# Another order for a fused RWKV-6 and feed-forward kernel

## The chip, the cores and the metric

The kernel runs on one core of one Trainium2 chip. The metric is the device time of one execution in microseconds, the median of several runs. A core has a matmul engine (PE, with its weight loads shown apart as PEld), a vector engine (DVE), a scalar engine (ACT), a further vector-like engine (POOL) and a queue that issues the transfers (SP). Each of them works through its own list in order; semaphores tie the lists together.

## What is computed

Two stages. The first is a linear attention with a decaying state: for each batch (4) and head (8) and each of 768 time steps, with vectors of length 48,

```python
cur   = einsum('bhd,bhe->bhde', u * k_t, v_t)
y_t   = einsum('bhd,bhde->bhe', r_t, state + cur)
state = w_t * state + einsum('bhd,bhe->bhde', k_t, v_t)
```

The second takes the 3072 tokens of 8 x 48 = 384 values and computes `maximum(x @ w1, x @ w2) @ w_out`, with 1024 inner columns.

## The kernel before

The time axis is cut into three segments of 256 steps, and the work into eight **units**: units 0 to 3 are segment 0 of one batch each, units 4 and 5 segment 1 of two batches each, units 6 and 7 segment 2 of two batches each. A unit's state feeds the unit of the next segment (0 and 1 feed 4, 2 and 3 feed 5, 4 feeds 6, 5 feeds 7).

A unit's chain, by the names that the order uses: `load` brings r, k, v, w. `wp` multiplies neighbouring decays, `ln` takes the logarithm, `ex` sums it along time on PE (from unit 3 on with the value split into two half-precision parts by `hi` and `lo`), `mz`, `e0` and `ie` make from it the factors that scale r and k. `rw`, `kw` weight r and k by the neighbour's decay; `scale.u.0` makes the scaled r, `scale.u.1` the scaled k. `rk`, `ru`, `dg`, `dd`, `di` make the diagonal term with u. The scaled r and k are turned by PE and copied back (`tr`, `te`: units 0 to 4) or by a DMA transpose (`dt`: units 5 to 7). `sc` multiplies k with r on PE in many small matmuls, `mk` is a masked copy of the result on DVE, `ya` multiplies it with v (rows of 32 small matmuls of 64x32), `yi` adds the state's part (12 or 24 small matmuls), `kv`, `st`, `sm`, `sb` update the state, `xe` copies the finished y out of PSUM as bf16 input of the second stage.

The second stage is rewritten: since `maximum(a, b) = relu(a - b) + b`, the kernel makes `wd = w1 - w2` (`wload`, then `wdiff` for each of three row blocks) and the product `w2 @ w_out` (`woload`, `wocast`, `w2turn`, `w2take`, `wfold`, `wctake`). Then `gt` is one PSUM bank of `x @ wd` (three matmuls of 512 columns, or six of 256 for units 0 to 3), `rl` its relu, `op` the output product of 128 tokens (11 matmuls of 384 columns), `oe` the copy out of PSUM, `os` the store. `hot` is a filler: matmuls on zeros, from the start's idle time.

There is no automatic scheduling. `ORDER` (line 53) is one written list of 652 entries; each is a function's name, the unit, further indices, and after `@` the engine where there is a choice (`d` DVE, `a` ACT, `p` POOL). The kernel calls the functions in that order (line 755), so it fixes the order within each engine's list, and by the buffers that rotate also who waits for which buffer. PSUM has four banks of the kind `G` (`ex`, `tr`, `gt`, `op`) and two double banks `Y` (`kv`, `sc`, `y`).

Lines that the steps touch: `hot` L234, `zero` L249 to L263, `w_diff` L176/L180, `w2_turn` L307, `load` L372, `ex` L395 to L398, `mz` L440, `dg` L502, `di` L516, `tr` L565, `dt` L582, `kv` L596, `sc` L641, `mk` L650, `yi` L675, `ya` L688, `gt` L706, `rl` L717/L719, `op` L725 and L729, `os` L743. Products and copies run through helpers at L176, L180 and L168.

Of the kernel before, what the change touches and what calls it, by code (L numbers as in the profile page):

```python
# [59 lines left out]
vb.0.0@p ln.2.0 we.1.0 ex.2.0 vb.0.1@a load.2.r scale.0.0.0.1@d di.0.0@d wload.1.0 te.0.0.0@a  # L60
wload.1.2 we.0.1 ie.1.0 rk.1.0@d kv.0 kw.1.0@d hot.8.4 tr.0.0.1 ru.1.0@d st.0.0@a dg.1
scale.1.1.0.0@p vb.1.1@a kv.1 e0.1.0 mz.2.0 scale.1.0.0.0@d dd.1@p te.0.0.1@a wload.0.2 st.1.0@a
tr.1.0.0 sb.1.1@a tr.1.0.1 ie.2.0 load.3.w.0 wload.0.0 sb.0.1@a zero.M.0@p rk.2.0@d st.0.1 wload.1.1
kw.2.0@p rw.2.0@d sc.0.0.1.0 st.1.1 zero.v.0@d w2turn.2.1 sb.0.0@a w2take.2.1@a e0.2.0 sc.0.0.0.0
di.1.0@d te.1.0.1@a scale.2.0.0.0@d sc.0.0.0.1 hot.8.1 mk.0.0.1.0 mk.0.0.0.0 sc.0.0.1.1 load.3.k
# [6 lines left out]
rl.1.3@a rl.0.3@a kw.3.0@p gt.1.1 gt.0.2 di.2.0@d rw.3.0@p rl.1.1@a vb.2.0@a gt.0.0 rl.0.0@a  # L72
mk.2.0.0.0 woload.2 kv.2 st.2.0@a rl.0.2@a sc.2.0.1.0 w2take.1.0@a sb.2.0@a sb.2.1@a ru.3.0@d gt.0.1
rl.0.1@a mk.2.0.1.0 woload.3 wocast.3@a gt.1.0 load.4.w.0 sm.1@p rl.1.0@a dg.3 wocast.1@p wocast.2@p
dd.3@p ex.3.0 mz.3.0 ie.3.0 e0.3.0 gt.1.2 rl.1.2@a di.3.0@d yi.2.0 ya.2.0.1.0 ya.2.0.0.0 wp.4.0@d
ln.4.0 hi.4@a wfold.1 wfold.2 wfold.0 wctake.1@a load.4.k scale.3.0.0.0@d scale.3.1.0.0@p tr.3.0.1
load.4.r load.3.v wctake.2@a st.2.1 wctake.0@a tr.3.0.0 rk.4.0@d te.3.0.1@a vb.3.1@p op.1.1
# [6 lines left out]
di.4.1@d mk.4.1.0.0 tr.4.0.0 gt.3.0 rl.2.1@a te.4.0.1@a mk.4.1.1.0 wp.5.0@p ln.5.0 gt.3.3 hi.5@a
lo.5@d load.5.r vb.4.0@p kv.4 st.4.0 rl.3.0@a gt.2.3 rl.3.3@a te.4.0.0@a rl.2.3@a gt.3.1 os.0.0
rk.5.0@p rk.5.1@p kw.5.0@p sb.4.1@a rw.5.0@p ru.5.0@d op.2.0 st.4.1 load.6.r oe.2.0@a sc.4.0.0.0
load.5.v sc.4.0.1.0 row.4 op.2.1 ex.5.0 sb.4.0@a di.4.0@d mk.4.0.1.0 rl.3.1@a ya.4.1.1.0 load.6.v
wl.4 ex.5.1 gt.3.2 mk.4.0.0.0 mz.5.0 oe.2.1@a e0.5.0 os.1.1 mz.5.1 wp.6.0@d scale.5.0.0.0@d load.6.k
# [12 lines left out]
rl.5.1@a sb.6.0@a dt.6.1.0 ex.7.0 mz.7.0 mk.6.1.0.0 rl.5.4@a ex.7.1 dt.6.0.0 mz.7.1 op.5.2 load.7.v
e0.7.0 sc.6.0.0.0 mk.6.0.0.0 sc.6.0.1.0 rk.7.1@p mk.6.0.1.0 ie.7.0 wl.5 os.3.0 op.5.3 rk.7.0@p
kw.7.0@p rw.7.0@d oe.5.2@a sb.6.1@a yi.6.0 ya.6.0.0.0 ya.6.1.0.0 scale.7.1.0.0@p os.5.2 dt.7.1.0
ya.6.1.1.0 ya.6.0.1.0 oe.5.3@a ru.7.0@d yi.6.1 e0.7.1 ru.7.1@p scale.7.0.0.0@d dt.7.0.0 op.5.1
vb.7.1@a xe.6.0@a xe.6.1@a dg.7 op.5.0 oe.5.1@a dd.7@a di.7.1@d oe.5.0@a os.4.2 scale.7.1.1.0@p
dt.7.1.1 gt.6.3 os.4.3 gt.6.4 os.5.0 gt.6.0 scale.7.0.1.0@d rl.6.0@a vb.7.0@d sc.7.0.1.0 gt.6.2
# [691 lines left out]
```

## Time and profile before

| | |
|---|---|
| median of three runs | 152.28 us (152.27 to 152.72) |
| the profiled execution | 151.69 us |
| its span, first to last instruction | 150.0 us |
| PE busy | 137.2 us |
| DVE busy | 115.9 us |
| POOL busy | 93.9 us |
| ACT busy | 89.8 us |
| moved by the DMA engines | 31.85 MB |

Line numbers in a row are those of the kernel; `out<-in` are the program's tile names; `x` is a count. A bracket at the end of a timeline row gives the idle time of that engine just before it, and what ended it; "issue" is idle time in which the engine waited for nothing that the profile shows. Matmuls overlap in PE, so distances from start to start say more than the duration of one. A row of a table of stretches gives for each engine the busy time and, in brackets, the number of its instructions, then the clock granted to PE.

### The profile page before, as it was taken

How to read it: one execution, taken by the hardware profiler on the slowest of the kernel's cores; microseconds unless marked ns; L12 is line 12 of the kernel's file. 1: busy time of each engine (PE TensorE's matmuls, PEld its weight loads, DVE VectorE, ACT ScalarE, POOL GpSimd, SP SyncE). 2: the span in 40 equal slices, each digit the busy share in tenths (PEclk: the TensorE clock that was granted, in tenths of full speed). 3: DMA queues.
4: the chain of work that ended last, by engine and by line, in shares of the span. 5: the costliest groups of instructions: out<-in, count | busy, mean ns of one | idle time of the engine just before them, and what ended most of it. 6: DMA issues, size and time to landing. Idle time of an engine off the chain costs nothing. (4 is left out here: it accounts for less than half of the span.)

```text
span 150.0 us, 5536 instructions
## 1 busy us (share of the span) xinstructions
PE 137.2 (91%) x2402; PEld 84.8 (57%) x2404; DVE 115.9 (77%) x155; ACT 89.8 (60%) x167; POOL 93.9 (63%) x110
## 2 busy tenths in 40 slices
...
GB/s 107 322 317 293 376 377 388 326 317 290 286 197 256 182 261 205 240 267 265 202 211 218 241 245 195 54 242 208 221 145 74 238 184 2 111 57 157 4 52 160
DMA packets 71187, 31.85 MB, mean 212 GB/s; under 512 B 66293, under 2 KB 70390, under 8 KB 71162
## 3 DMA queue, kind: packets, MB, share of 16 engines
...
q8 instruction: 19, 0.31, 1.0%
...
## 5 line engine op out<-in xcount | busy, mean ns | idle before, releaser
L706 PE MATMUL G<-xT,wd_sb 128*128 128x256 bf16 (+1 forms) x192 | 35.0, 329 | 0.7 <-DVE rp L176 0.6
L729 PE MATMUL G<-wo_sb,gT 128*128 128x384 bf16 x192 | 35.1, 326 | 0.0
L650 DVE CAST_PREDICATED M<-mask,Y 128x1024 bf16<-128x1024 int32 (+1 forms) x26 | 28.7, 1132 | 5.3 <-PE Y L641 4.9
L717 ACT ACTIVATE gT<-G 128x512 bf16<-128x512 f32 x41 | 23.2, 599 | 14.1 <-PE G L706 13.9
L729 PEld LDWEIGHTS <-gT 128*128 128x128 bf16 x192 | 18.8, 98 | 12.4
L706 PEld LDWEIGHTS <-wd_sb 128*128 128x128 bf16 x192 | 18.3, 99 | 13.2 <-issue 1.3
L180 POOL TENSOR_TENSOR rku<-rku,u_b 128x384 f32<-128x384 f32 x12 | 15.7, 1330 | 3.6 <-DVE rku L176 3.6
L180 POOL TENSOR_TENSOR kp<-lk,iE 128x384 bf16<-128x384 f32 x16 | 16.3, 1038 | 2.6 <-ACT iE L460 1.5
L725 PE MATMUL G<-wc_sb,xT 128*128 128x384 bf16 x72 | 15.7, 328 | 0.0
L234 PE MATMUL G<-S_b 128*128 128x512 bf16 x46 | 12.8, 424 | 2.5 <-DVE S_b L263 2.1
L168 ACT COPY RK<-G 128x1024 bf16<-128x1024 bf16 x12 | 11.7, 1012 | 3.2 <-PE G L565 3.2
L168 ACT CAST xT<-Y 128x768 bf16<-128x768 f32 x8 | 8.1, 1029 | 7.6 <-PE Y L688 4.6
L688 PE MATMUL Y<-M,vp 64*32 64x128 bf16 x768 | 9.9, 223 | 2.9 <-issue 2.9
L641 PE MATMUL Y<-RK 48*64 48x128 bf16 x384 | 9.7, 225 | 2.8 <-DMA RK<-kp 1.8
L502 DVE TENSOR_REDUCE dg<-rku 128x16 f32<-128x768 f32 x12 | 11.1, 948 | 1.0 <-POOL rku L180 0.7
L168 ACT CAST S_b<-S_f 64x192 bf16<-64x192 f32 (+1 forms) x15 | 8.6, 574 | 4.6 <-DVE S_f L612 4.3
L641 PEld LDWEIGHTS <-RK 48*64 48x64 bf16 x384 | 6.3, 108 | 8.0 <-issue 4.6
L688 PEld LDWEIGHTS <-vp 64*32 64x32 bf16 x768 | 7.4, 91 | 5.6 <-issue 4.8
L176 POOL TENSOR_TENSOR S_f<-T,W 128x192 f32<-128x192 f32 (+1 forms) x6 | 4.4, 738 | 8.9 <-ACT W L488 8.9
L516 DVE TENSOR_TENSOR M<-identq,gd 128x512 int32<-128x512 int32 x12 | 9.7, 810 | 0.3 <-ACT gd L168 0.3
L234 PEld LDWEIGHTS <-S_b 128*128 128x128 bf16 x48 | 5.0, 107 | 8.6 <-issue 2.6
L176 DVE TENSOR_TENSOR rp<-lr,G 128x768 bf16<-128x768 f32 (+2 forms) x11 | 8.7, 800 | 0.8 <-POOL lk L180 0.7
...
## 6 DMA issues: line engine op xcount, KB each, us to landing
lk<-in_k_dram SPq DMA_DIRECT2D x12, 384.0 KB, 5.2
lv<-in_v_dram SPq DMA_DIRECT2D x12, 384.0 KB, 6.4
lr<-in_r_dram SPq DMA_DIRECT2D x10, 384.0 KB, 5.3
lw<-in_w_dram SPq DMA_DIRECT2D x9, 384.0 KB, 4.4
...
gT<-in_moe_w_dram SPq DMA_DIRECT2D x4, 512.0 KB, 8.9
...
wso<-in_moe_w_out_dram SPq DMA_DIRECT2D x4, 384.0 KB, 6.2
```

The source lines that it names most:

```text
L168: (nc.scalar.copy if e == "a" else nc.vector.tensor_copy if e == "d" else nc.gpsimd.tensor_copy)(o, i)
L176: op(o, a, b)
L180: op(o[:, g], a[:, g], b[:, g])
L234: nc.tensor.matmul(t, zz[:, 0:P], zz[:, 0:512], start=True, stop=True)
L502: nc.vector.reduce_sum(s.dg[:, b].rearrange("p i h -> p h i"), s.rku[:, b], axis=AX.X)
L641: nc.tensor.matmul(t[q * Q:(q + 1) * Q, e, p * P:(p + 1) * P].rearrange("s (i g) -> s i g", i=2), s.kT[d, b, j, y * n + p, q, :], s.rT[d, ...
L650: nc.vector.copy_predicated(t[:, :, 2 * n * y:2 * n * (y + 1)].rearrange("s i (p e) g -> s p e i g", e=2), mask[:, j].bitcast(I32).unsquee ...
L688: nc.tensor.matmul(lhsT=s.vp[g, b, 2 * p + e, j, m * 32:(m + 1) * 32], rhs=s.M[b, j][g, :, 2 * p + e, :], **into(s, b, q, p * 96 + (e + m) ...
L706: nc.tensor.matmul(t[:, m * n * P:(m + 1) * n * P].rearrange("c (b t) -> c b t", t=P), wd_sb[:, ko, fo * P:(fo + 1) * P], s.xT[:, 0:n, ko, :],
L717: nc.scalar.activation(o, i, AF.Relu)
L725: nc.tensor.matmul(t[:, 0:HD], s.xT[:, a, ko, :], wc_sb[:, ko, :], start=(ko == 0), stop=False)
L729: nc.tensor.matmul(t[:, 0:HD], s.gT[:, c:c + P], wo_sb[:, f, :], start=False, stop=(f == FO - 1))
```

## The change

Only `ORDER` is replaced. All 652 entries are there again, with the same names and indices; their sequence differs from the first entry on, the loads included, and 66 entries carry another engine letter: 13 go from POOL to DVE, 8 from DVE to POOL, 17 from ACT to DVE, 15 from DVE to ACT, 5 from ACT to POOL and 8 from POOL to ACT. In several places `op` or `gt` entries now stand between the `yi` and `ya` rows of a unit (for instance `op.2.1` and `op.3.0` among those of unit 4, `op.4.2` and `op.4.3` between `yi.5.0` and `yi.5.1`). The lists, cut to the parts that are spoken of:

```diff
 ORDER = """
-load.0.r load.0.k zero.r@d zero.s.1@p zero.s.0@d zero.M.1@p load.0.w.1 ident zero.m@p hot.8.2 mask
-zero.k.1@p load.0.w.0 tri wp.0.1@d rw.0.1@d wp.0.0@d ln.0.0 hot.8.3 ex.0.0 identb@p rk.0.0@d
-load.1.w.0 u zero.o@p uspread kw.0.1@d mz.0.0 ln.0.1 ex.0.1 mz.0.1 utake@a ru.0.0@d load.1.k
...
-ya.0.0.1.0 wload.0.1 woload.0 load.2.v zero.M.2@p ya.0.0.0.0
-w2take.0.1@a wocast.0@p wdiff.1@d ya.1.0.0.0 yi.1.0 ln.3.0 ya.1.0.1.0 load.3.r w2turn.1.0 vb.2.1@p
-xe.1.0@a sm.0@p woload.1 yi.0.0 ya.0.0.0.1 zero.v.2@d row.2 w2take.1.1@a ru.2.0@d ya.0.0.1.1
-xe.0.0@a dg.2 hi.3@a sc.2.0.0.0 trih@a gt.1.3 lo.3@d w2turn.0.0 gt.0.3 dd.2@a w2take.0.0@a rk.3.0@d
...
-sc.3.0.0.0 mz.4.0 kv.3 e0.4.0 gt.2.0 mz.4.1 st.3.0@a ru.4.1@p sb.3.0@a op.0.1 load.4.v mk.3.0.0.0
-rl.2.0@d sc.3.0.1.0 scale.4.0.0.0@d ie.4.0 e0.4.1 scale.4.0.1.0@d op.1.0 wl.3 oe.0.1@a oe.1.0@a
-kw.4.0@p scale.4.1.0.0@p we.3 wl.2 gt.2.2 load.6.w.0 ru.4.0@p st.3.1 we.2 scale.4.1.1.0@d tr.4.1.1
-te.4.1.1@a sm.2@p tr.4.1.0 te.4.1.0@a vb.4.1@p op.0.0 ya.3.0.0.0 mk.3.0.1.0 ya.3.0.1.0 dg.4 oe.0.0@d
...
-ru.5.1@p rl.3.2@a dg.5 vb.6.1@a ie.5.0 op.3.0 scale.5.1.0.0@p yi.4.0 yi.4.1 dt.5.0.0 dd.5@p ln.6.0
-ya.4.0.0.0 ya.4.0.1.0 xe.4.0@a ya.4.1.0.0 xe.4.1@d oe.3.0@a e0.5.1 row.5 os.1.0 os.0.1 hi.6@a op.3.1
-gt.4.5 vb.5.1@a scale.5.1.1.0@p scale.5.0.1.0@d os.2.1 rl.4.5@a gt.4.4 oe.3.1@a di.5.1@d lo.6@d
-gt.4.3 gt.4.2 gt.4.0 rl.4.4@a dt.5.1.0 sc.5.0.1.0 we.4 sm.4@p sc.5.0.0.0 rl.4.3@a rl.4.0@a dt.5.0.1
...
-ya.5.0.0.0 sc.5.1.0.0 op.4.2 scale.6.0.0.0@d ie.6.0 e0.6.1 mk.5.1.0.0 wp.7.0@p yi.5.1 load.7.k
-yi.5.0 ya.5.1.0.0 ya.5.0.1.0 scale.6.0.1.0@d dt.6.0.1 ya.5.1.1.0 op.4.1 dg.6 load.7.r xe.5.1@d
...
+load.0.w.0 zero.m@p zero.o@p load.1.w.0 tri zero.s.0@d hot.8.2 hot.8.3 load.0.r mask ident wp.0.0@p
+ln.0.0 ex.0.0 rw.0.0@d zero.M.1@p zero.k.0@d zero.k.1@p u uspread zero.v.2@d load.0.w.1 wp.0.1@d
+wp.1.0@d ln.1.0 rw.0.1@d load.0.k rk.0.0@d mz.0.0 ln.0.1 ex.0.1 utake@a hot.8.0 mz.0.1 ie.0.1
+load.0.v vb.0.0@d identq@a identb@p kw.0.1@p wt.0.0 e0.0.1 ex.1.0 wt.0.1 ru.0.0@d zero.r@d load.1.k
+zero.s.1@p kw.1.0@d hot.8.5 load.2.w.0 dg.0 vb.0.1@a ie.0.0 kw.0.0@p we.0.0 e0.0.0 scale.0.1.0.0@p
...
+te.1.0.0@a sc.1.0.1.0 st.1.1 woload.2 scale.2.0.0.0@d sm.1@d row.2 wload.0.1 wp.3.0@p kw.2.0@p
+sb.0.1@a scale.2.1.0.0@p tr.2.0.0 tr.2.0.1 wocast.2@a w2turn.2.0 sc.1.0.0.0 te.2.0.1@a sb.1.1@d
+w2turn.1.1 w2take.1.1@a te.2.0.0@a di.1.0@d mk.1.0.1.0 ya.1.0.1.0 yi.1.0 mk.1.0.0.0 wdiff.1@d
+ya.1.0.0.0 ya.0.0.0.1 ya.0.0.1.1 woload.1 wload.0.2 wocast.1@a wdiff.2@d w2turn.1.0 ru.2.0@d dg.2
+xe.1.0@a load.3.r zero.M.2@p ya.0.0.1.0 ln.3.0 yi.0.0 wdiff.0@p gt.1.2 w2take.2.0@a load.2.v
+load.3.k gt.1.3 ya.0.0.0.0 w2take.1.0@a gt.1.0 rl.1.3@d hi.3@p lo.3@d sc.2.0.1.0 woload.3 sm.0@d
+vb.2.0@a vb.2.1@p rl.1.2@a dd.2@a gt.1.1 xe.0.0@a trih@a gt.0.2 ex.3.0 rk.3.0@d rl.1.1@a rl.1.0@a
...
+rl.0.0@a wl.2 mz.4.1 e0.4.1 ya.2.0.1.0 rk.4.1@d vb.3.0@p kv.3 op.0.1 ya.2.0.0.0 mz.4.0 st.3.0@a
+sb.3.0@a sb.3.1@a st.3.1 we.2 rw.4.0@d scale.4.0.1.0@d kw.4.0@d ie.4.0 oe.0.1@a ru.4.0@p sm.2@p
+xe.2.0@a op.1.1 gt.2.0 e0.4.0 scale.4.0.0.0@d sc.3.0.1.0 load.5.w.0 scale.4.1.1.0@d oe.1.1@a
+ru.4.1@p load.4.v vb.4.1@p wp.5.0@p vb.4.0@a sc.3.0.0.0 mk.3.0.0.0 gt.2.2 rl.2.2@a op.1.0 tr.4.1.0
+ya.3.0.0.0 te.4.1.0@a ln.5.0 tr.4.1.1 oe.1.0@a mk.3.0.1.0 ya.3.0.1.0 te.4.1.1@a row.4 hi.5@a yi.3.0
...
+load.6.v rk.5.1@d wl.4 mk.4.0.0.0 mk.4.0.1.0 rl.2.3@a op.2.0 oe.2.0@a gt.3.2 ie.5.0 ya.4.1.0.0 we.4
+op.2.1 rl.3.2@a e0.5.1 e0.5.0 ya.4.0.0.0 wp.6.0@d ya.4.0.1.0 ya.4.1.1.0 load.6.k rk.5.0@p rw.5.0@p
+scale.5.0.1.0@d vb.5.1@a op.3.0 load.6.r oe.2.1@a yi.4.0 kw.5.0@p scale.5.1.0.0@p vb.5.0@a yi.4.1
+ln.6.0 hi.6@a xe.4.0@a xe.4.1@a scale.5.0.0.0@d ru.5.1@d ru.5.0@d op.3.1 dg.5 gt.4.6 gt.4.4 dt.5.0.0
+oe.3.1@d dd.5@a gt.4.7 rl.4.6@a di.5.0@d sm.4@p gt.4.0 dt.5.1.0 sc.5.0.0.0 sc.5.0.1.0 rl.4.7@a
...
+rl.4.3@a op.4.0 oe.4.0@d sc.5.1.0.0 sb.5.1@a mk.5.1.0.0 ya.5.0.0.0 yi.5.0 mz.6.0 mz.6.1 vb.6.1@a
+ie.6.0 e0.6.1 load.7.k os.1.0 rw.6.0@p ru.6.0@d e0.6.0 load.7.r op.4.2 op.4.3 dg.6 yi.5.1 kw.6.0@p
+scale.6.1.1.0@p ya.5.1.1.0 ya.5.0.1.0 ya.5.1.0.0 oe.4.3@d os.2.0 scale.6.0.0.0@d dt.6.1.1
...
+gt.7.4 rl.7.4@a gt.7.6 rl.7.6@a gt.7.3 rl.7.3@a gt.7.5 rl.7.5@d op.7.2 oe.7.2@a os.7.2 op.7.3
+oe.7.3@a op.7.1 oe.7.1@d op.7.0 oe.7.0@d os.7.3 os.7.1 os.7.0
 """.split()
```

More of the change, by code (lines that the diff above doesn't have):

```diff
@@ L60 @@
[L60 to L65, printed above, removed]
@@ L66 @@
-mk.0.0.1.1 zero.v.1@d te.1.0.0@a sc.1.0.0.0 scale.2.1.0.0@p tr.2.0.0 mk.0.0.0.1 sb.1.0@a wdiff.2@p
-tr.2.0.1 te.2.0.1@a mk.1.0.0.0 w2turn.1.1 te.2.0.0@a wdiff.0@p sc.1.0.1.0 mk.1.0.1.0 w2turn.0.1
-w2turn.2.0 w2take.2.0@a wp.3.0@d ya.0.0.1.0 wload.0.1 woload.0 load.2.v zero.M.2@p ya.0.0.0.0
-w2take.0.1@a wocast.0@p wdiff.1@d ya.1.0.0.0 yi.1.0 ln.3.0 ya.1.0.1.0 load.3.r w2turn.1.0 vb.2.1@p
-xe.1.0@a sm.0@p woload.1 yi.0.0 ya.0.0.0.1 zero.v.2@d row.2 w2take.1.1@a ru.2.0@d ya.0.0.1.1
-xe.0.0@a dg.2 hi.3@a sc.2.0.0.0 trih@a gt.1.3 lo.3@d w2turn.0.0 gt.0.3 dd.2@a w2take.0.0@a rk.3.0@d
@@ L72 @@
[L72 to L77, printed above, removed]
@@ L84 @@
[L84 to L88, printed above, removed]
-ru.5.1@p rl.3.2@a dg.5 vb.6.1@a ie.5.0 op.3.0 scale.5.1.0.0@p yi.4.0 yi.4.1 dt.5.0.0 dd.5@p ln.6.0
@@ L101 @@
[L101 to L106, printed above, removed]
@@ new lines @@
+zero.v.0@d load.1.r scale.0.0.0.0@d mz.1.0 wt.1.0 scale.0.1.0.1@p ie.1.0 load.2.r rk.1.0@d wp.2.0@d
+kv.0 load.2.k st.0.0@a we.1.0 dd.0@p di.0.0@d zero.M.0@p wload.1.0 rw.1.0@d sb.0.0@a tr.0.0.0 e0.1.0
+te.0.0.0@a load.1.v hot.8.4 ru.1.0@d we.0.1 w2turn.0.1 w2take.0.1@a sc.0.0.0.0 scale.0.0.0.1@d
+tr.0.0.1 ln.2.0 scale.1.1.0.0@p sc.0.0.1.0 dg.1 load.3.w.0 scale.1.0.0.0@d tr.1.0.1 vb.1.1@d
+te.0.0.1@a st.0.1 rk.2.0@d ex.2.0 mz.2.0 mk.0.0.0.0 vb.1.0@p mk.0.0.1.0 sc.0.0.1.1 wload.1.2
+w2turn.0.0 te.1.0.1@a w2take.0.0@d tr.1.0.0 sc.0.0.0.1 mk.0.0.1.1 e0.2.0 ie.2.0 w2turn.2.1
@@ new lines @@
+w2take.2.1@a dd.1@a kv.1 st.1.0@a sb.1.0@a wload.0.0 hot.8.1 mk.0.0.0.1 wload.1.1 rw.2.0@p
+te.1.0.0@a sc.1.0.1.0 st.1.1 woload.2 scale.2.0.0.0@d sm.1@d row.2 wload.0.1 wp.3.0@p kw.2.0@p
[3 more added lines that the diff above has]
+xe.1.0@a load.3.r zero.M.2@p ya.0.0.1.0 ln.3.0 yi.0.0 wdiff.0@p gt.1.2 w2take.2.0@a load.2.v
@@ new lines @@
+load.3.k gt.1.3 ya.0.0.0.0 w2take.1.0@a gt.1.0 rl.1.3@d hi.3@p lo.3@d sc.2.0.1.0 woload.3 sm.0@d
+vb.2.0@a vb.2.1@p rl.1.2@a dd.2@a gt.1.1 xe.0.0@a trih@a gt.0.2 ex.3.0 rk.3.0@d rl.1.1@a rl.1.0@a
+kw.3.0@p di.2.0@d mk.2.0.1.0 rl.0.2@a sc.2.0.0.0 mk.2.0.0.0 mz.3.0 woload.0 wocast.0@a rw.3.0@p
+gt.0.3 ru.3.0@d load.4.w.0 rl.0.3@a wocast.3@p gt.0.1 rl.0.1@a wp.4.0@d kv.2 st.2.0@a dg.3 load.3.v
+e0.3.0 scale.3.0.0.0@d ie.3.0 zero.v.1@d wfold.0 wfold.2 wfold.1 st.2.1 sb.2.0@a sb.2.1@a load.4.r
+scale.3.1.0.0@p tr.3.0.1 wctake.0@a dd.3@d ln.4.0 hi.4@a row.3 wctake.2@a wctake.1@a vb.3.1@a
@@ new lines @@
+te.3.0.1@a yi.2.0 lo.4@d di.3.0@d tr.3.0.0 load.4.k te.3.0.0@a ex.4.0 rk.4.0@d gt.0.0 ex.4.1
+rl.0.0@a wl.2 mz.4.1 e0.4.1 ya.2.0.1.0 rk.4.1@d vb.3.0@p kv.3 op.0.1 ya.2.0.0.0 mz.4.0 st.3.0@a
[3 more added lines that the diff above has]
+ya.3.0.0.0 te.4.1.0@a ln.5.0 tr.4.1.1 oe.1.0@a mk.3.0.1.0 ya.3.0.1.0 te.4.1.1@a row.4 hi.5@a yi.3.0
@@ new lines @@
+dg.4 dd.4@d wl.3 di.4.0@d xe.3.0@a scale.4.1.0.0@p we.3 op.0.0 oe.0.0@d gt.2.1 tr.4.0.1 sc.4.1.1.0
+sc.4.1.0.0 di.4.1@d load.5.k gt.3.3 load.5.r rl.2.0@a rl.2.1@a tr.4.0.0 te.4.0.1@a load.6.w.0
+te.4.0.0@a os.0.0 lo.5@d mk.4.1.1.0 load.5.v gt.3.0 rl.3.0@a rl.3.3@a mk.4.1.0.0 kv.4 st.4.0 ex.5.1
+ex.5.0 sm.3@p mz.5.1 sb.4.0@a gt.3.1 gt.2.3 rl.3.1@a st.4.1 sc.4.0.1.0 sb.4.1@d mz.5.0 sc.4.0.0.0
+load.6.v rk.5.1@d wl.4 mk.4.0.0.0 mk.4.0.1.0 rl.2.3@a op.2.0 oe.2.0@a gt.3.2 ie.5.0 ya.4.1.0.0 we.4
+op.2.1 rl.3.2@a e0.5.1 e0.5.0 ya.4.0.0.0 wp.6.0@d ya.4.0.1.0 ya.4.1.1.0 load.6.k rk.5.0@p rw.5.0@p
```

35 lines of the change are left out of this document (17 added, 18 removed).

## The prediction

> **What bounds the kernel now.** I read the page first, then the stretches between landmarks, then PE's waits, then the timeline around each.
>
> ```profile
> span 150.0 us, 5536 instructions
> PE 137.2 (91%) x2402; PEld 84.8 (57%) x2404; DVE 115.9 (77%) x155; ACT 89.8 (60%) x167; POOL 93.9 (63%) x110
> ...
> q8 instruction: 19, 0.31, 1.0%
> ```
>
> ```profile
> core 0: us, PE busy (x) PEld busy (x) DVE busy (x) ACT busy (x) POOL busy (x), PEclk, DMA share, GB/s
> 6.22:31.20 24.98, 22.35 (x336) 14.14 (x337) 23.87 (x44) 16.23 (x38) 19.89 (x26) 1.00 1.12 341
> 31.20:60.20 29.00, 27.74 (x448) 19.35 (x447) 24.93 (x32) 22.98 (x45) 21.21 (x23) 0.94 0.97 249
> 60.20:146.80 86.60, 82.92 (x1609) 49.73 (x1608) 66.17 (x80) 48.78 (x83) 47.42 (x46) 1.00 0.72 166
> 146.80:150.00 3.20, 0.00 (x0) 0.00 (x0) 0.00 (x0) 0.48 (x1) 0.00 (x0) 0.84 0.50 184
> ```
>
> Two regimes. From 6.22 (the first product of w) to 31.20 (the last weight difference) DVE is the full engine: 23.87 of 24.98 us. From 60.20 (the first `ya` of unit 3) to 146.80 it is PE: 82.92 of 86.60, while DVE has 20 us to spare. The last 3.20 us are the last copy and its store. PE's real waits after the start are three:
>
> ```profile
> 35.38 1.26 PE L706 MATMUL G<-xT,wd_sb 128*128 128x256 bf16 x6
> 60.22 0.75 PE L688 MATMUL Y<-M,vp 64*32 64x128 bf16 x64
> 83.65 0.64 PE L641 MATMUL Y<-RK 48*64 48x128 bf16 x32 [1.81 <-DMA RK<-kp]
> 96.97 0.31 PE L688 MATMUL Y<-M,vp 64*32 64x128 bf16 x14 [1.07 <-issue]
> 118.73 0.81 PE L706 MATMUL G<-xT,wd_sb 128*128 128x512 bf16 x3 [0.65 <-DVE rp L176]
> ```
>
> 1.81 us for a DMA transpose of unit 5, 1.07 us for nothing that the profile shows ("issue") inside unit 5's `ya` rows, 0.65 us for a PSUM bank that DVE held. Together 3.53 us.
>
> **What "issue" is.** The same wait stands in the start, also inside a `ya` row:
>
> ```profile
> 32.36 0.40 PE L688 MATMUL Y<-M,vp 64*32 64x128 bf16 x26 [1.83 <-issue]
> ...
> 0.00:32.10 32.10, 26.50 (x346) 15.72 (x349) 25.74 (x48) 17.52 (x39) 26.16 (x44) 1.00 1.04 313
> 0.00:96.70 96.70, 88.08 (x1625) 57.16 (x1628) 83.00 (x113) 67.25 (x128) 79.79 (x97) 0.98 0.96 256
> 0.00:26.30 26.30, 22.27 (x220) 12.39 (x222) 19.94 (x38) 14.19 (x34) 20.36 (x39) 1.00 1.03 311
> 0.00:74.00 74.00, 68.00 (x1115) 45.16 (x1118) 63.31 (x91) 51.19 (x102) 60.27 (x77) 0.98 1.01 274
> 0.00:76.30 76.30, 70.30 (x1241) 46.84 (x1245) 65.47 (x94) 53.48 (x104) 62.57 (x79) 0.98 1.00 271
> ```
>
> Queue q8 moves 0.31 MB in 19 pieces, 16 KB each; 4,806 PE and weight-load records over 19 are 253 for a piece. At the first stall 346+349 = 695 records had run, at the second 1625+1628 = 3253: the distance is 2558, ten times 256 less two. So I read the stalls as PE running out of instructions at the end of a block of 256. Block ends then lie at 695 and every 256 records before and after it. The block before the first stall began at record 439, just before 26.30 (442), so it lasted 6.1 us to 32.36. The block before the second began at 2997, when the `yi` row at 94.19 started; it lasted 2.8 us to 96.97. One block ran through without a wait in 2.3 us (records 2231 at 74.00 to 2487 at 76.30), so there is no fixed limit; I use 2.8 us where the loads are light and 6.1 us in the start.
>
> A rule speaks against this reading. The Trainium skill, Runtime: NRT & Kernel Launch, section Instruction fetch mechanics, has the same blocks of 256 instructions, but calls their refill hidden, since instructions are dispatched more slowly than they are filled. The trace agrees on the size, and shows two stalls of 1.83 and 1.07 us where it expects none. By the page the second is something else and stays in the new order: that is a rival below.
>
> **The change, part by part.** No instruction is added or removed: both orders have the same 652 entries, and PE has the same matmuls. What changes is position, and the engine of 66 entries.
>
> *Engines.* With the row means of before, 30 entries move onto DVE (13 from POOL, 17 from ACT) with 20.3 us, 23 leave it with 16.6: DVE 115.9 becomes some 119.6. POOL loses some 13 us, ACT gains some 3.
>
> *Instruction blocks.* Counting the new PE order in the same way, the block with unit 5's rows now holds most of `op.4.2`, all of `op.4.3`, then `yi.5.1` and three `ya` rows: 0.9+1.9+0.4+1.1 = 4.3 us at least (`op` from the rows below, 92.30 to 94.19; 32 `ya` matmuls 0.36 us, 91.59 to 91.95), against 2.8 needed. Unit 4's block holds `op.3.0` between its rows, 3.2 us. So the 1.07 us go.
>
> ```profile
> 91.59 0.42 PE L688 MATMUL Y<-M,vp 64*32 64x128 bf16 x32
> 91.95 0.42 PE L641 MATMUL Y<-RK 48*64 48x128 bf16 x16
> 92.30 0.66 PE L725 MATMUL G<-wc_sb,xT 128*128 128x384 bf16 x3
> 92.80 1.46 PE L729 MATMUL G<-wo_sb,gT 128*128 128x384 bf16 x8
> 94.19 0.86 PE L675 MATMUL Y<-RK,S_b 128*32 128x128 bf16 x48
> ```
>
> *Transposes.* On SP `dt.5.1.0` stood behind `row.5` and three stores; now it follows `dt.5.0.0` directly.
>
> ```profile
> 75.18 1.75 SPq L582 DMA_TRANSPOSE RK<-rp  x1
> 76.98 0.41 SPq L472 DMA_DIRECT2D row<-MZ  x1
> 77.44 1.26 SPq L743 DMA_DIRECT2D out_dram<-osb  x2
> 78.82 1.29 SPq L743 DMA_DIRECT2D out_dram<-wb  x1
> 80.22 1.26 SPq L582 DMA_TRANSPOSE RK<-kp  x1
> ```
>
> It was issued at 80.22 and let PE go at 83.65, 3.4 us later. Its place in the new order is worked out after the next part.
>
> ```profile
> lk<-in_k_dram SPq DMA_DIRECT2D x12, 384.0 KB, 5.2
> ...
> gT<-in_moe_w_dram SPq DMA_DIRECT2D x4, 512.0 KB, 8.9
> ```
>
> *Loads.* Counted in pieces of these two sizes, the last feed-forward weight now has 8.64 MB ahead and with it instead of 8.25; 0.39 MB at 341 GB/s are 1.1 us. DVE, not this load, is later (below), so I cost it at nothing; uncovered it is 1.1 us.
>
> *The start, by DVE.* The first feed-forward matmul needs all of `wdiff`. DVE's first need is now `load.0.r`, with 0.2+0.4+0.4 MB before and in it; that is what stood before and in the half of w that started DVE at 6.22, so it starts there again. From its row means the old list to `wdiff.1` (38 entries) sums to 25.9 us and took 24.98; the new one to `wdiff.2` (43 entries, `wdiff.2`, two more `vb`, a `w2take`, `sm.1` and `sb.1.1` among them) sums to 28.3. In the old proportion, 28.3 x 24.98/25.9 = 27.3: done at 33.5. Without any wait 28.3 x 23.87/25.9 = 26.1: 32.3. The first `gt` follows at 33.5 rather than 35.38.
>
> *The middle, by DVE.* What I did not expect to find: between that point and PE's `ya.3.0.0.0` the new order puts more on DVE than on PE.
>
> ```profile
> 29.99 1.21 DVE L176 TENSOR_TENSOR wd_sb<-gT 128x1024 bf16<-128x1024 f32 x1
> 36.35 0.56 DVE L413 SCALAR_TENSOR_TENSOR wst<-lg,wst 128x384 f16<-128x384 f32 x1 [2.66 <-ACT wst L200]
> 51.01 1.02 DVE L440 TENSOR_TENSOR MZ<-G,lg 128x384 f32<-128x384 f32 x2 [0.36 <-PE G L396]
> 51.95 1.22 DVE L650 CAST_PREDICATED M<-mask,Y 128x1024 bf16<-128x1024 int32 x1
> ```
>
> ```profile
> L502 DVE TENSOR_REDUCE dg<-rku 128x16 f32<-128x768 f32 x12 | 11.1, 948 | 1.0 <-POOL rku L180 0.7
> L176 DVE TENSOR_TENSOR rku<-lr,lk 128x768 f32<-128x768 f32 x8 | 8.6, 1079 | 0.0
> ```
>
> With the means of the view by shape (two of its rows stand here), the 22 entries of before from 31.20 to the end of `mk.3.0.0.0` at 53.17 sum to 19.7 us; less its waits of about 3.2 the stretch took 18.8 (factor 0.95). PE needed that mask only at 60.22, so DVE was 7 us early. Now 30 entries lie there (`kw.4.0`, both scalings of r and one of k of unit 4, a `rl`, `sm.0`, `st.3.1` and more ahead of the mask): 25.4 x 0.95 = 24.1 us. The mask ends at 33.5+24.1 = 57.6, with 0.7 us of waits (the old ones without the 2.66, whose cause, `hi.3` on ACT, moves to POOL) at 58.3. PE's own work between the first `gt` and `ya.3.0.0.0` is 22 us (the old 24.84 us for what was 2.3 more, `op.0.0` and a `tr`, and partly at a lower clock): it arrives near 55.5 and waits. So the start's gain is eaten: at 58.3 PE stands 2.3 us of work earlier in its list than before at 60.22.
>
> *From there to the end.* Before: 146.80-60.22 = 86.58, less 3.53 of waits 83.05, plus the 2.3 us not yet done: 85.35. `dt.5.1.0` is issued after `scale.5.0.0.0`, 20 DVE entries or 17.3 us after 58.3, plus 1.3 us for `dt.5.0.0`: 76.9, landing 80.3. PE took 83.65-1.81-60.22 = 21.6 us from the first `ya` of unit 3 to the `sc` row that waited; the new list has the 2.3 us more and one `gt` (some 0.7) less, so it comes at 58.3+23.2 = 81.5: no wait, margin about 1 us. For waits of PE on DVE I take 1.7 us: what PE waited for DVE in all of before, by these rows, bounded by 0.4 us (`mk.3.0.1.0` follows the first mask, 1.2 us against 0.8 us of PE work) and 3.5 (all that was won).
>
> ```profile
> PE Y L641 <- DVE M L650: 0.7, 1, 0.7
> PE G L706 <- DVE rp L176: 0.6, 1, 0.6
> PE Y L641 <- DVE T L615: 0.4, 1, 0.4
> ```
>
> *Sum.* 58.3 + 85.35 + 1.7 + 3.2 (the tail; its last copy goes to DVE, within 0.1 us) = 148.55, against the span of 150.0: 1.45 us less. The profiled execution took 151.69, so 150.2; the median of the runs is 152.28, 0.6 above it, so **150.8**. Its own range, with DVE's waits from 0 to 1.5 us, is 149.6 to 151.9.
>
> **The rivals.**
>
> *DVE loses nothing:* no waits in start or middle. The mask ends at 32.3+24.1 = 56.4, with 0.4 of waits later: 56.4+85.35+0.4+3.2 = 145.35, so 147.6. For it: DVE stood 95% full there before. Against: it waited 3.2 us in the middle even so.
>
> *The transposes are late again:* the margin of 1 us is lost and the 1.81 us return: 152.6, no change. For it: in both orders `dt.5.1.0` stands right before the `sc` rows that read it, with four `gt` ahead now and five then. Against: no store stands between the two transposes any more.
>
> *The page's rule:* the 1.07 us were unit 5's rows themselves and not instructions: 151.9, no change. Against it stands the distance of 2558 records.
>
> *Slower: DVE is the bound from the start to unit 3.* Every wait of DVE up to `mk.3.0.0.0` is now paid in full, since PE stands behind that mask. With the 3.2 us of before, and 0.5 us because a block end now falls into `ya.0.0.0.1` (that block begins near 26.8, plus 6.1 is 32.9, then 1.5 us of PE work to the first `gt`, which `rl.1.3` on DVE awaits): 33.5+0.5+24.1+3.2 = 61.3, end 151.55, so 153.8. It decides from 2.2 us of waits on. For it: the lists above, and the clock row, 0.94 granted between 31.20 and 60.20 after a stall of that kind. Against: 2.66 of the 3.2 had a cause that moves.
>
> **How the numbers follow.** A run of this kernel can't be told from no change within 0.3%, 151.8 to 152.7. Chances: forecast 0.42, no waits 0.14 (faster, 0.56); late transposes 0.13 and the page's rule 0.06 (same, 0.19); DVE the bound 0.25 (slower). The range leaves out the ends: 147.9 to 153.9.
>
> **What would show it.** Right: no "issue" wait of PE over 0.3 us after 40 us; no wait of PE on RK near 80; a PE wait of 1 to 3 us on DVE's mask before the first `ya` of unit 3, near 56 to 59; first `gt` between 33 and 35; DVE near 119.6 busy. Wrong: the first `gt` after 36, a wait for `wd_sb` on a load, or PE waits for DVE above 3 us in the second half.

## The result, and the profile after

| | runs | median, us | lowest to highest, us |
|---|---|---|---|
| before | 6 | 152.28 | 151.78 to 152.72 |
| after | 6 | 150.38 | 149.82 to 151.65 |

The new order takes 0.9892 of the time of the old one, with a 95% interval of 0.9846 to 0.9937: 1.6 us, or 1.9 between the medians. The forecast was 150.8. Now and then an execution of a kernel is disturbed and takes a per cent or more longer: ratios, here and below, leave these executions out and medians keep them, so the two need not agree.

Beware of setting the two profiles side by side. The profiled execution of before (151.69 us, span 150.0) was faster than all of its six runs, that of after (151.65 us, span 149.8) the slowest of its six. The spans differ by 0.2 us where the medians differ by 1.9. What they can show is where the time lies, and there they differ a lot. First the page of after, then its stretches, cut where PE starts the first `ya` of unit 3 (60.22 before, 60.13 here) and where PE ends.

```profile
span 149.8 us, 5513 instructions
PE 139.4 (93%) x2402; PEld 84.7 (56%) x2404; DVE 118.8 (79%) x162; ACT 93.4 (62%) x168; POOL 85.4 (57%) x98
```

```profile
6.32:35.17 28.85, 25.05 (x367) 15.51 (x367) 27.34 (x49) 18.06 (x38) 18.48 (x21) 0.92 0.98 308
0.00:34.30 34.30, 28.82 (x346) 16.59 (x348) 27.17 (x49) 18.83 (x38) 23.88 (x42) 0.95 0.93 287
0.00:62.30 62.30, 55.98 (x858) 34.77 (x860) 53.07 (x83) 41.28 (x82) 43.13 (x60) 0.95 0.93 267
60.13:146.60 86.47, 85.06 (x1629) 51.00 (x1627) 67.38 (x81) 54.16 (x90) 44.43 (x42) 1.00 0.80 179
```

DVE's total of 118.8 us is close to the 119.6 that was counted. From the first `ya` of unit 3 to PE's end it took 86.47 us against 86.58 before, but with some 2.3 us more work in it. So the second half won some 2.2 us, and in these two profiles the start lost about as much: PE came to unit 3 at the same moment with 2.3 us less behind it.

The timeline of PE in after shows both. Columns are start, us, what ran, and in brackets the idle time before it and what ended that.

```profile
31.83 0.43 PE L688 MATMUL Y<-M,vp 64*32 64x128 bf16 x32 [1.24 <-DVE M L650]
...
32.96 0.48 PE L688 MATMUL Y<-M,vp 64*32 64x128 bf16 x34 [0.42 <-DVE M L650]
34.41 0.82 PE L688 MATMUL Y<-M,vp 64*32 64x128 bf16 x30 [0.97 <-issue]
...
37.09 1.66 PE L706 MATMUL G<-xT,wd_sb 128*128 128x256 bf16 x12
...
60.13 0.42 PE L688 MATMUL Y<-M,vp 64*32 64x128 bf16 x32
...
62.38 0.23 PE L675 MATMUL Y<-RK,S_b 128*32 128x128 bf16 x1 [0.64 <-issue]
...
84.38 0.64 PE L641 MATMUL Y<-RK 48*64 48x128 bf16 x32
...
92.51 0.65 PE L725 MATMUL G<-wc_sb,xT 128*128 128x384 bf16 x3
...
94.29 0.65 PE L725 MATMUL G<-wc_sb,xT 128*128 128x384 bf16 x3
...
96.63 1.03 PE L688 MATMUL Y<-M,vp 64*32 64x128 bf16 x96
97.60 0.66 PE L725 MATMUL G<-wc_sb,xT 128*128 128x384 bf16 x3
...
103.89 0.64 PE L641 MATMUL Y<-RK 48*64 48x128 bf16 x32 [0.36 <-DMA RK<-rp]
```

The first `gt` came at 37.09, 1.7 us later than before, not 1.9 us earlier as forecast. Ahead of it PE waited 1.24 and 0.42 us for DVE's masks and 0.97 us for instructions, at record 346+348 = 694. From there to 60.13 PE waited no more than 0.16 us at a time, and the forecast wait for unit 3's mask isn't there. The wait for the transpose (84.38) and the issue wait in unit 5's rows (96.63, all 96 matmuls in one piece) are gone. One issue wait of 0.64 us is new, at record 858+860 = 1718, in unit 3's `yi` row. With 0.36 us at 103.89 and 0.32 us at 125.98 the second half has 1.3 us of waits instead of 3.53.

### The profile page after: what moved, and what is told of

Its sections match the earlier page's. It is cut to its first block, busy times and chain, and to the rows that moved or that the text cites. A ratio compares the mean times of both kernels' runs of the same rounds, so it can differ in the third digit from the quotient of the medians.

```text
span 149.8 us, 5513 instructions
## 1 busy us (share of the span) xinstructions
PE 139.4 (93%) x2402; PEld 84.7 (56%) x2404; DVE 118.8 (79%) x162; ACT 93.4 (62%) x168; POOL 85.4 (57%) x98
## 4 chain that ended last, share of the span: by engine, by line
PE 75%; DVE 13%; DMA 6%; issue 3%; ACT 1%; DVEq 0%; ACTq 0%
PE G L729 20%; PE G L706 17%; PE G L725 8%; PE G L234 6%; DMA RK<-rp 6%; PE Y L688 6%; PE Y L641 4%; DVE M L650 3%; PE G L565 3%; PE Y L675 3%; PE Y L596 2%; DVE M L516 1%; DVE rp L176 1%; PE G L395 1%; DVE dg L502 1%
## 5 line engine op out<-in xcount | busy, mean ns | idle before, releaser
L706 PEld LDWEIGHTS <-wd_sb 128*128 128x128 bf16 x192 | 17.8, 98 | 12.2 <-POOL wst L202 0.2
L180 POOL TENSOR_TENSOR kp<-lk,iE 128x384 bf16<-128x384 f32 x14 | 15.6, 1135 | 2.7 <-ACT iE L460 1.5
L234 PE MATMUL G<-S_b 128*128 128x512 bf16 x46 | 15.0, 479 | 2.1 <-DVE S_b L263 1.8
L168 ACT CAST xT<-Y 128x768 bf16<-128x768 f32 x10 | 9.9, 1023 | 5.2 <-PE Y L688 4.2
L180 POOL TENSOR_TENSOR rku<-rku,u_b 128x384 f32<-128x384 f32 x8 | 10.0, 1269 | 2.5 <-DVE rku L176 2.5
L234 PEld LDWEIGHTS <-S_b 128*128 128x128 bf16 x48 | 5.5, 120 | 9.2 <-issue 4.9
L719 DVE TENSOR_SCALAR gT<-G 128x512 bf16<-128x512 f32 x8 | 5.5, 687 | 6.1 <-PE G L706 6.1
L168 ACT COPY osb<-G 128x384 f32<-128x384 f32 x11 | 5.3, 479 | 7.4 <-PE G L729 6.6
L641 PE MATMUL Y<-RK 48*64 48x128 bf16 x384 | 8.9, 220 | 0.8 <-DMA RK<-rp 0.7
L460 ACT ACTIVATE iE<-MZ 128x768 f32<-128x768 f32 (+2 forms) x9 | 5.6, 627 | 5.7 <-DVE MZ L440 5.7
```

The lines of the kernel that those rows point to most:

```text
L168: (nc.scalar.copy if e == "a" else nc.vector.tensor_copy if e == "d" else nc.gpsimd.tensor_copy)(o, i)
L180: op(o[:, g], a[:, g], b[:, g])
L234: nc.tensor.matmul(t, zz[:, 0:P], zz[:, 0:512], start=True, stop=True)
L641: nc.tensor.matmul(t[q * Q:(q + 1) * Q, e, p * P:(p + 1) * P].rearrange("s (i g) -> s i g", i=2), s.kT[d, b, j, y * n + p, q, :], s.rT[d, ...
L706: nc.tensor.matmul(t[:, m * n * P:(m + 1) * n * P].rearrange("c (b t) -> c b t", t=P), wd_sb[:, ko, fo * P:(fo + 1) * P], s.xT[:, 0:n, ko, :],
```

## The experiments

Two theories stood against each other. **M**: the gain lies in the second half, and the start gained nothing. **S**: the start is the gain, and the profiled execution of after was an odd one.

**The changed kernel once more.** No edit.

> The changed kernel once more, to see whether its first profiled execution (first gt at 37.09 us, not 33.5) is typical. Theory M (the start gained nothing or little, the gain comes from the second half, where 3.5 us of PE waits became about 1.3): median near 150.4 us, first gt at 34 to 37 us, from the first ya of unit 3 to the last matmul again 86.0 to 86.6 us. Rival S (the start is the gain, and the profiled execution was an odd one): first gt at 33 to 34.5 us in this profile, span near 148.0.

149.94 us (12 runs) against 151.64 for before on that chip (29 runs), ratio 0.9907 (0.9868 to 0.9946). The profiled execution was a median one this time (149.96 us). From its page, stretches and PE timeline:

```profile
span 148.2 us, 5515 instructions
...
59.87:144.90 85.03, 84.75 (x1629) 50.72 (x1627) 67.22 (x81) 53.98 (x90) 44.66 (x41) 1.00 0.78 179
```

```profile
33.91 0.51 PE L688 MATMUL Y<-M,vp 64*32 64x128 bf16 x30 [0.16 <-issue]
...
36.13 2.36 PE L706 MATMUL G<-xT,wd_sb 128*128 128x256 bf16 x12
...
59.87 0.42 PE L688 MATMUL Y<-M,vp 64*32 64x128 bf16 x32
```

The first `gt` comes at 36.13, later than before again, so S falls; the span of 148.2 us, which S had too, comes from the second half. The second half takes 85.03 us with 84.75 of PE work: here all of its waits are gone, 0.64 at unit 3 too. M missed with its 86.0 to 86.6 us, which had those waits in them; they are the 1.4 us between the two profiles. So an issue wait at one and the same instruction can be there in one execution and not in the next.

**Half of the change at a time.** The order is cut at the first `ya` of unit 3: entries ahead of it from one kernel, what is left in the order of the other.

```diff
 headB_tailA: before's ORDER up to the cut, then after's
- ... vb.4.1@p op.0.0 ya.3.0.0.0 mk.3.0.1.0 ya.3.0.1.0 dg.4 oe.0.0@d sb.3.1@a rl.2.2@a yi.3.0 ...
+ ... vb.4.1@p op.0.0 sb.3.1@a wp.5.0@p vb.4.0@a rl.2.2@a ya.3.0.0.0 ln.5.0 mk.3.0.1.0 ya.3.0.1.0 row.4 ...
 headA_tailB: after's ORDER up to the cut, then before's
```

> Before's order up to the first ya of unit 3, then what is left in after's order. Theory M: start as before (first gt near 35.4, first ya of unit 3 near 60.2), no wait on the transposes at 80 to 84 us, no issue wait in unit 5's rows; 1.8 to 2.2 us faster than before: 150.1 to 150.5 us. Rival S: the tail is worth little; 151.7 to 152.3 us.

> After's order up to the first ya of unit 3, then what is left in before's order. Theory M: the waits of the second half come back (the transpose about 1.8 us, a block end in unit 5's rows about 1.0 us) and the start gains nothing: 152.0 to 154.0 us. Rival S: the start keeps its gain: 150.2 to 151.0 us.

All four on the same chip, medians in us:

| | tail of before | tail of after |
|---|---|---|
| head of before | 151.64 | 151.07, ratio 0.9963 (0.9919 to 1.0007) |
| head of after | 153.28, ratio 1.0156 (1.0098 to 1.0214) | 149.94 |

Behind after's head the tail is worth 3.3 us by the medians and 3.8 by the ratios. The head, with the tail of before, costs 1.6 us by the medians and 2.4 by the ratio. Both hit M (with the tail of after the two heads can't be told apart, since the intervals overlap). The profile of before was itself late in the start: behind the same head the first `gt` came at 34.41 us here and at 34.13 to 34.51 in three more profiles and at 35.78 in one, behind after's head at 36.13 to 37.09 in three. And the view of waits of headA_tailB shows the old waits back (columns: total, times, longest):

```profile
PE Y L641 <- DMA RK<-kp: 1.5, 1, 1.5
...
PE Y L688 <- issue: 0.8, 1, 0.8
```

But headB_tailA missed: 0.6 us (nothing to 1.2 by the interval) instead of 1.8 to 2.2. PE's timeline says where the rest went:

```profile
62.48 1.44 PE L706 MATMUL G<-xT,wd_sb 128*128 128x256 bf16 x6 [2.29 <-DVE osb L168]
```

PE waited 2.29 us for a bank that `oe.0.0` on DVE had to copy out. I took this for a slip of the splice and tried to mend it.

```diff
- op.0.0 sb.3.1@a wp.5.0@p ... dd.4@d di.4.0@d xe.3.0@a oe.0.0@d gt.2.1
+ op.0.0 sb.3.1@a oe.0.0@a wp.5.0@p ... dd.4@d di.4.0@d xe.3.0@a gt.2.1
```

> Before's order up to the first ya of unit 3, then after's, with oe.0.0 now on ACT behind sb.3.1 instead of on DVE behind di.4.0. Theory M: the 2.29 us that PE waited for that copy at 62.48 us shrink to 0 to 0.6 us and stay away; span near 147.3 us, 2 to 3 us faster than before and faster than the changed kernel. Rival (new order loads DVE so that any PE gain ahead of unit 4 is waited away again): PE waits near 62 to 68 us for masks of unit 4 instead, no faster than the changed kernel.

Ratio 0.9948 (0.9910 to 0.9987): within the intervals nothing was won over the run without the edit. The rival was right, though the wait was for another tile:

```profile
64.14 0.42 PE L641 MATMUL Y<-RK 48*64 48x128 bf16 x16 [2.36 <-ACT xT L168]
```

The edit did not make this wait: ACT copied that `xT` from 63.06 to 64.06 us before it and from 63.09 to 64.09 after it, so it had only stood behind the first one. The tail of after is laid out for a PE that arrives later. A PE that comes with 2.3 us more of its list done waits them away ahead of unit 4. How much of after's tail could be had with before's head stays open.

**The transpose alone.**

```diff
- row.5 os.1.0 os.0.1 ... rl.4.4@a dt.5.1.0 sc.5.0.1.0
+ row.5 dt.5.1.0 os.1.0 os.0.1 ... rl.4.4@a sc.5.0.1.0
```

> Before with dt.5.1.0 alone moved, ahead of the three stores that stood before it on SP. Theory M: the wait on RK near 83 us (1.81 us in the first profile of before) is below 0.3 us and nothing takes its place ahead of unit 5; 1.0 to 1.8 us faster than before. Rival: the time is waited again at the next thing that is late (unit 5's rows, the bank at 118 us); less than 0.6 us faster.

Ratio 0.9929 (0.9892 to 0.9965), 0.5 to 1.6 us: the lower part of what M expects. The profiled execution took 154.25 us against the median of 150.27, so only this is read from it: PE has no wait on RK in it.

**Unit 5's rows alone, in three ways.** First with `op.4.1`:

```diff
- yi.5.0 ya.5.1.0.0 ya.5.0.1.0 ... ya.5.1.1.0 op.4.1 dg.6
+ yi.5.0 op.4.1 ya.5.1.0.0 ya.5.0.1.0 ... ya.5.1.1.0 dg.6
```

> Before with op.4.1 alone moved up, between yi.5.0 and ya.5.1.0.0. Theory of the instruction blocks: the block that ends in unit 5's rows now holds 1.9 us more PE work, so the 1.07 us issue wait goes and nothing else changes: about 151.2 us, 0.9 to 1.1 us faster than before. The rule that refills are hidden (the wait is the rows' own): an issue wait of about 1 us stays in unit 5's rows, 152.3 us.

Ratio 0.9975 (0.9927 to 1.0023): no gain that can be measured. The issue wait went as the block theory says, and another took its place in PE's timeline:

```profile
98.33 2.12 PE L706 MATMUL G<-xT,wd_sb 128*128 128x512 bf16 x9 [1.13 <-ACT wb L168]
```

So I moved the copy that frees this bank, and the transpose with it:

```diff
- row.5 os.1.0 ... dt.5.1.0 sc.5.0.1.0
+ row.5 dt.5.1.0 os.1.0 ... sc.5.0.1.0
- yi.5.0 ya.5.1.0.0 ... op.4.1 dg.6 ... oe.4.2@d xe.5.0@a ... oe.4.1@a
+ yi.5.0 op.4.1 ya.5.1.0.0 ... dg.6 ... oe.4.2@d oe.4.1@a xe.5.0@a ...
```

> Before with three entries moved: op.4.1 between yi.5.0 and ya.5.1.0.0, oe.4.1 (the copy that frees its bank) ahead of xe.5.0 on ACT, and dt.5.1.0 ahead of the three stores on SP. Theory M (the gain of the change is the waits of the second half, and each can be taken away singly): the issue wait in unit 5's rows is gone, the wait of 1.13 us for ACT's copy that replaced it when op.4.1 alone was moved is below 0.3 us, the wait on RK near 83 us is below 0.5 us; 2.0 to 2.8 us faster than before, as fast as the whole new order. Rival: each wait gives way to the next thing that is late; less than 1 us faster.

Ratio 0.9935 (0.9890 to 0.9981), no more than the transpose alone:

```profile
97.35 2.12 PE L706 MATMUL G<-xT,wd_sb 128*128 128x512 bf16 x9 [1.14 <-DVE xT L168]
```

`gt.5.7` now waits as long for its own operand, the copied rows of unit 5. In before, `op.4.1` stood behind the last `ya` and hid both copies. So a third try broke the rows with `op.4.2` instead:

```diff
- sc.5.1.0.0 op.4.2 scale.6.0.0.0@d ... yi.5.1 load.7.k yi.5.0 ya.5.1.0.0
+ sc.5.1.0.0 scale.6.0.0.0@d ... yi.5.1 load.7.k yi.5.0 op.4.2 ya.5.1.0.0
```

> Before with dt.5.1.0 moved as in the run above and op.4.2, not op.4.1, put between yi.5.0 and ya.5.1.0.0, so that op.4.1 still stands between unit 5's last ya and gt.5.7. Theory M in its mended form (op.4.1 hid the copies that gt.5.7 needs; a filler is needed in the rows and another behind them): no issue wait in unit 5's rows and no wait at gt.5.7; 2.0 to 2.8 us faster than before, at least 0.5 us faster than with dt.5.1.0 alone. Rival: a wait of about 1 us comes back somewhere between 93 and 100 us; no faster than with dt.5.1.0 alone.

Ratio 0.9957 (0.9915 to 1.0000). The rival again: `op.4.2` had hidden DVE's mask. PE also waited 0.54 us for the transpose at 82.82, so moving `dt.5.1.0` does not always take that wait away whole.

```profile
92.92 0.86 PE L675 MATMUL Y<-RK,S_b 128*32 128x128 bf16 x48 [1.38 <-DVE M L650]
...
96.97 0.31 PE L688 MATMUL Y<-M,vp 64*32 64x128 bf16 x14 [0.34 <-issue]
```

My theory that each wait can be taken away singly falls for the rows. Every `op` in that place already covers something: the mask, the copies, or the instruction transfer. The new order has two `op` ahead of the last rows of unit 5 and one behind them (92.51, 94.29 and 97.60 in after's timeline), and none of the three waits stands there.

**Are the issue waits instruction blocks?** 64 instructions are added, near 23 us.

```diff
-    def hot(n, _):
+    def hot(n, x):
...
+        if x == 1:
+            for _ in range(32):
+                nc.tensor.matmul(t[:, 0:32], zz[:, 0:P], zz[:, 0:32], start=True, stop=True)
```

> Before with 32 small matmuls (128x32, 64 instructions with their weight loads) added to hot.8.1 near 23 us; nothing else. Block theory: the issue waits stay at the same count of instructions, so they move 64 instructions, 32 matmuls, ahead in the work: the first from after the 6th matmul of ya.1.0.1.0 to about the 18th of ya.1.0.0.0, the one of unit 5 from after the 82nd of its 96 ya matmuls to after the 50th. If the waits belong to the rows themselves (the rule that refills are hidden): they stay at the same matmuls, the 6th and the 82nd.

One run, 150.54 us. From its timeline and stretches (the two numbers with x behind PE and weight loads count the records so far; the edit moves the lines behind it down by three, so L691 is `ya`, L310 `w2_turn`):

```profile
29.58 0.95 PE L691 MATMUL Y<-M,vp 64*32 64x128 bf16 x51
30.99 0.30 PE L691 MATMUL Y<-M,vp 64*32 64x128 bf16 x13 [0.46 <-issue]
...
36.36 0.55 PE L310 MATMUL G<-osb,gT 128*128 128x128 f32 x3 [1.91 <-issue]
```

```profile
0.00:30.80 30.80, 27.58 (x347) 16.64 (x349) 24.80 (x45) 17.23 (x39) 24.36 (x42) 1.00 1.04 309
0.00:36.20 36.20, 31.05 (x475) 19.03 (x477) 29.53 (x52) 20.70 (x45) 27.61 (x45) 1.00 1.04 313
0.00:113.30 113.30, 105.17 (x2009) 67.03 (x2011) 99.68 (x132) 78.95 (x147) 90.62 (x107) 1.00 0.98 249
```

The first wait moved to behind the 51st of 64 matmuls, which is the 19th of `ya.1.0.0.0` (18th expected), at record 696. The others stand at 952 and 4020: 256 and 13 x 256 - 4 records behind it. The one at 36.36 isn't in a `ya` row at all, but in a turned weight block, and the last one, of 0.69 us at 113.50, is in an `op`. The wait in unit 5's rows was to move to their 50th matmul and wasn't there: the block's end was, and its instructions had come in time (they landed at 93.46 us, PE got there at 95.2). In b_tail2 the issue waits stand at records 695, 1207 and 3763, again whole blocks apart but for four. So the place of these waits goes by the count and not by the rows. That they are waits for instructions, the packed traces show directly: they hold the 16 KB pieces of queue q8 one by one, and each of the 22 issue waits of PE after 20 us, in all the profiles, ended 1.2 to 1.6 us after one of these pieces had landed (in before, pieces at 30.96 and 95.71, ends at 32.36 and 96.97). The rule in the Trainium skill (Runtime: NRT & Kernel Launch, Instruction fetch mechanics), that the fetch is hidden, doesn't hold here: the traces have waits of 0.16 to 2.32 us at block ends. It calls the crossing "mostly hidden" as well, and most block ends do pass without a wait.

**What holds up the start.** Three entries that the change had moved from ACT to DVE were taken off it again, all ahead of the masks that PE waits for at 31.83.

```diff
- tr.1.0.1 vb.1.1@d    ... te.1.0.1@a w2take.0.0@d ... te.2.0.1@a sb.1.1@d
+ tr.1.0.1 vb.1.1@p    ... te.1.0.1@a w2take.0.0@a ... te.2.0.1@a sb.1.1@a
```

> After with three entries taken off DVE ahead of the masks that PE waits for at 31.8 us: vb.1.1 to POOL, w2take.0.0 and sb.1.1 to ACT, 1.4 us of DVE work. Theory D (DVE sets the first gt): the 1.24 us wait at the first ya goes, the first gt comes 1.3 to 2 us earlier, at 34.2 to 35 us; 1 to 2 us faster than the changed kernel. Theory F (the block of instructions that ends in ya.0.0.0.1 sets it: it began near 28 us and such blocks took 5.4 to 6.4 us in the starts seen so far): PE reaches the block's end earlier and waits there, the issue wait grows from 0.16 to 0.97 us to 1.3 to 2.2 us, and the first gt stays at 35.5 to 37 us; the same time as the changed kernel, within 0.5 us.

147.88 us (147.42 to 148.60, 6 runs), ratio to before 0.9781 (0.9728 to 0.9835): 1.9 us below the changed kernel if that is taken at its 0.9907. D is right and F wrong:

```profile
31.08 0.42 PE L688 MATMUL Y<-M,vp 64*32 64x128 bf16 x32
...
32.18 1.12 PE L688 MATMUL Y<-M,vp 64*32 64x128 bf16 x64 [0.39 <-DVE M L650]
...
34.55 1.47 PE L706 MATMUL G<-xT,wd_sb 128*128 128x256 bf16 x12
...
57.48 0.42 PE L688 MATMUL Y<-M,vp 64*32 64x128 bf16 x32
...
81.28 0.64 PE L641 MATMUL Y<-RK 48*64 48x128 bf16 x32 [0.47 <-DMA RK<-kp]
```

The wait for the first mask is gone, and no issue wait of F's size came instead. The block's end lies inside the row at 32.18; there 0.34 us pass between two starts, 1.4 us after the block's piece had landed, so the instructions were the next bound already. The first `gt` is 1.58 us earlier than in the second profile of after. That and 0.89 us on the clock of those twelve matmuls (2.36 to 1.47), less the 0.47 us at 81.28, are the 2.0 us between the two spans (148.2 and 146.2). That the clock is part of the edit's doing isn't shown, but it is not the whole gain: at mean clocks of 0.986 to 0.989 two executions of a_dve took 148.4 and 148.6 us, six of after 149.0 to 151.1. Then the dose was raised:

```diff
- load.0.v vb.0.0@d ... zero.v.0@d load.1.r
+ load.0.v vb.0.0@a ... zero.v.0@p load.1.r
```

> The changed kernel with the three entries taken off DVE as before and two more: vb.0.0 to ACT (it took 1.2 to 1.5 us on DVE) and zero.v.0 to POOL (0.34 us). Theory D, DVE still sets the first gt: it comes at 33 to 34 us instead of 34.55, and the kernel is another 0.5 to 1.5 us faster. Rival P, PE's own list has become the bound there (it had 0.39 us of waits left between 29 and 34.55 us): the first gt stays at 34.2 to 34.8 us and the time is that of the run with three entries, within 0.4 us.

147.75 us (146.10 to 149.20, 6 runs), ratio 0.9705 (0.9637 to 0.9773). The two intervals overlap, and the spans of the profiled executions are 146.2 us both; no further gain is shown.

```profile
30.79 0.48 PE L688 MATMUL Y<-M,vp 64*32 64x128 bf16 x34 [0.38 <-DVE M L650]
33.03 0.51 PE L688 MATMUL Y<-M,vp 64*32 64x128 bf16 x30 [1.75 <-issue]
...
34.61 1.48 PE L706 MATMUL G<-xT,wd_sb 128*128 128x256 bf16 x12
```

DVE was 1.4 us earlier at this mask, PE reached the end of the block as much sooner, and waited there until 33.03. The first `gt` stayed, as rival P had it, but for another reason than P gave: not PE's list, the instructions. The start has two bounds within 2 us of each other.

## Why the prediction was right, and where it was wrong

The time was right: 150.38 us against 150.8. Two of its steps were wrong by amounts that nearly cancelled, so the number is in part luck. By one of its own signs, a first `gt` after 36, its account of the start was wrong.

**Right: the transposes, the block reading, the end.** SP's rows of after show the two of unit 5 directly behind one another:

```profile
78.20 1.55 SPq L582 DMA_TRANSPOSE RK<-rp  x1
79.86 1.27 SPq L582 DMA_TRANSPOSE RK<-kp  x1
```

`dt.5.1.0` went out at 79.86 and not 76.9, and PE came to the `sc` row at 84.38 and not 81.5: both some 2.9 us later than forecast, so the margin held. It was thin: PE waited 0.47 us there in a_dve. b_dt puts 0.5 to 1.6 us on this one move. The block reading is shown by b_shift and by the pieces of q8, and the rival by the page's rule falls. The work from unit 3 to PE's end was forecast as 85.35 us without waits; the second profile of after has 85.03 with 84.75 busy.

**Wrong: "the start, by DVE".** The step "in the old proportion, 28.3 x 24.98/25.9 = 27.3: done at 33.5" mis-sized DVE's list. It took 28.85 us, from 6.32 to 35.17, of which 27.34 busy; 26.1 had been counted as busy. Two entries make up more than the difference, in DVE's timeline of after:

```profile
9.86 1.17 DVE L168 CAST vp<-lv 128x384 bf16<-128x384 f32 x1
...
21.26 0.35 DVE L168 CAST vp<-lv 128x384 bf16<-128x384 f32 x1
...
28.79 1.65 DVE L516 TENSOR_TENSOR M<-identq,gd 128x512 int32<-128x512 int32 x1
...
33.95 1.22 DVE L176 TENSOR_TENSOR wd_sb<-wst 128x1024 bf16<-128x1024 f32 x1
```

The same cast took 0.35 us later, and the `M` row 0.68 us in a_dve: here they took 0.82 and 0.97 us more. The step also named the wrong event, as before's own rows could have told: there DVE was done with the weight differences at 31.20, and the first `gt` came 4.2 us later. The first `gt` followed PE's rows behind the masks, and these waited for DVE earlier in the list than `wdiff.2`. a_dve shows it: 1.4 us of entries off DVE ahead of the masks bring the first `gt` to 34.55.

**Wrong: "the middle, by DVE".** The mask of unit 3 was to end at 58.3 and PE to wait 1 to 3 us for it. PE was never there in time to wait. It came at 60.13 and not near 55.5, since the first `gt` was late and the work between it and unit 3 took 23.0 us and not 22. DVE's list was sized too long as well: from 35.17 to the end of the mask at 59.62 (the first of the two below) it was busy for 22.35 us, where 24.1 had been counted. So the mask was done half a microsecond before PE came:

```profile
58.41 2.34 DVE L650 CAST_PREDICATED M<-mask,Y 128x1024 bf16<-128x1024 int32 x2
```

With the first `gt` at 34.55 in a_dve, PE comes at 57.48 and still doesn't wait there: the mask is done at 56.97, again half a microsecond ahead. So DVE bounds the start, but not the middle, if only by that half microsecond, and the slower rival fails by the same step. Its two details were there (a block end in `ya.0.0.0.1`, 0.97 us, and `rl.1.3` on DVE waiting 1.82 us for `gt.1.3`), but PE did not stand behind that DVE list.

**Wrong in size: waits of PE on DVE in the second half, 1.7 us.** There were none; of 1.3 us in the first profile, all are issue and transposes. The statement "no issue wait of PE over 0.3 us after 40 us" failed with the 0.64 at record 1718. By the same count of 256 (695 + 4 x 256 = 1719) I could have seen it: I had followed the blocks through units 4 and 5 only.

**The sum.** Forecast 58.3 + 87.05 (85.35 and 1.7 of waits) + 3.2. Measured 60.13 + 86.47 + 3.2 in the first profile, 59.87 + 85.03 + 3.3 in the second. The start was 1.6 to 1.8 us too early, the second half 0.6 to 2.0 us too long. The stated range, 149.6 to 151.9, doesn't follow from its reason: with 0.7 us of DVE's waits in the sum, waits of 0 to 1.5 give 150.1 to 151.6. A time that comes out right doesn't vouch for its terms.
